# A new order for the opening of a fused attention and gated MLP kernel

## The chip, the cores and the metric

The kernel runs on one core of one Trainium2 chip. The metric is device time in microseconds (us), from a launch's start to its end. The profile is one execution; its engines are PE (TensorE, with PEld for its weight loads), DVE (VectorE), ACT (ScalarE), POOL (GpSimd) and SP (SyncE, which here only issues DMAs).

## The reference

Sliding-window causal attention over 8 batches, 8 heads, 576 positions and head size 64, then an MLP with the gate h·cos(h) on its result:

```python
scores = scale * np.matmul(q, k.transpose(0, 1, 3, 2))
rel = pos[:, None] - pos[None, :]
scores = np.where((rel >= 0) & (rel < 64), scores, -1e9)
attn = softmax(scores)                     # last axis
x = np.matmul(attn, v)                     # to (4608 tokens, 512)
h = x @ w_in                               # 512 -> 2048
return (h * np.cos(h)) @ w_out             # 2048 -> 512, float32
```

## The kernel before, in words

**Tiles.** The 4608 tokens are nine MLP tiles of 512 (`mt`). Tile 0 is positions 0 to 511 of batch 0; tile 1 takes the rest of batch 0 and most of batch 1. From tile 1 on, a loop gives PE its matmuls (L458, L611) and a list of due times (`at`, `pump`) fits in the attention of the next batch. Everything up to there, the opening, is an order written out by hand: the string `FIRST` (L44), which is split at blanks, each word being one step. Each engine executes its own instructions in that order and waits at a step until what it reads has come and what it overwrites is free.

**The steps**, by their letters (the numbers after a letter are a head pair p of 0 to 3 and a half g of tile 0, unless said otherwise; a last letter d, a, p or s is the engine that does it: DVE, ACT, POOL or SP):

- `Lq0.p`, `Lk0.p`: load q, k of batch 0, pair p, cast to bf16 by a DMA issued by POOL (L149). Pair 0 comes by SP in float32 (L155) and is cast by `cq`, `ck`. `Lq1`, `Lk1` load batch 1. `Lv0.c` loads rows of v, 128 positions each (L172); `Lwi`, `Lwo` load quarters of w_in and w_out (L188, L191).
- `io` makes the iota for the masks on POOL (L127), `mk` the masks in five DVE steps (L131 to L135), `mc` casts them to bf16 in three steps on ACT (L139).
- `tq.p`, `tk.p`: 18 small PE transposes of a pair (L200) into PSUM; `pq`, `pk` copy that to SBUF. `Tq`, `Tk`, `Pq`, `Pk` are the same for batch 1.
- `s.p.g.bank`: PE writes the mask into a PSUM bank and adds the scores of four 64-row blocks (L304, L311). `m`: the row max on DVE (L321). `e`: four exps on ACT (L338). `i`: reciprocal on DVE (L348). `n`: the product with it, `w`, on POOL or DVE (L355). `w`: PE transposes it (L371). `c`: copy to SBUF (L121). `Gs`, `Gm`, `Ge` and so on are the same for the groups of batch 1 (there the max and the mask are one DVE operation, L326).
- `zA`, `zB`, `zC`: v is wanted in 128-row windows that begin every 64 rows, so each odd window is put together from halves of the even ones, by a copy between partitions: either an engine's copy (L121) or a DMA from SP (L183). `zA.0`, `zA.1` make the window that half 0 of tile 0 needs, `zB.0`, `zB.1` two that half 1 needs, `zC` one for later.
- `v.a.g`: attention times v for pairs 2a, 2a+1 (L408); `x.a.g` copies that to `xT`, the MLP's input (L121).
- `h.g.f.bank`: the h job f of 0 to 7, eight matmuls (L422). `S` is the sine on ACT (L428), `g` the gate on DVE (L434). `tb` loads ACT's table for it (L453). An h job of half 0 needs x.0.0 and x.1.0; one of half 1 needs x.0.1 and x.1.1.

**Resources that order the steps.** Five single PSUM banks (the last number of `s`, `Gs` and `h`) are taken in turn: a step waits until the bank's last reader is done. Three more PSUM slots (`ps_t`) are shared by tq, tk, Tq, Tk, w and v steps in the order of allocation, so a step waits for the copy that frees the slot three allocations back. A POOL DMA issue waits, on its queue, for the landing of the one eight issues before it.

The copy of v between partitions, with its choice of engine, and the place where FIRST is run:

```python
if engine == "s":
    nc.sync.dma_start(out=to, in_=of)
else:
    copy(engine, to, of)
...
for step in FIRST.split():
    name, *args = step.split(".")
    steps[name](*[int(a) if a.isdigit() else a for a in args])
```

Of the kernel before, what the change touches and what calls it, by code (L numbers as in the profile page):

```python
# [10 lines left out]
def _safe_warn(msg, *a, **kw):  # L11
# [30 lines left out]


FIRST = (  # L44
# [18 lines left out]
)  # L63


# [1 line left out]
def kernel(  # L67
# [10 lines left out]
    B, H, S, D = q.shape  # L78
# [63 lines left out]
    def rows_tile(name):  # L142
        return ld.tile([128, NC * H * D], BF16, tag=name, name=name)

    def load_heads(name, b, p0=0, n=PAIRS):
        if (name, b) not in st:
            st[name, b] = rows_tile(name)[:, 0:PAIRS * RC * D].rearrange("p (a x) -> p a x", a=PAIRS)
        src = {"q": q, "k": k}[name][b, 2 * p0:2 * p0 + 2 * n]
        nc.gpsimd.dma_start(out=st[name, b][:, p0:p0 + n],  # L149
                            in_=src.rearrange("(a h) (p c) d -> (h p) a (c d)", h=2, c=RC))  # L150
# [6 lines left out]
    def cast_plain(name, engine):  # L157
        if (name, 0) not in st:
            st[name, 0] = rows_tile(name)[:, 0:PAIRS * RC * D].rearrange("p (a x) -> p a x", a=PAIRS)
        copy(engine, st[name, 0][:, 0], st.pop(("rows", name)))  # L160

    def load_chunk(name, b, c):
        if (name, b) not in st:
            st[name, b] = rows_tile(name)[0:NP].rearrange("p (c x) -> p c x", c=NC)
        src = {"q": q, "k": k}[name][b, :, c * NP:c * NP + NP]
        nc.gpsimd.dma_start(out=st[name, b][:, c].rearrange("p (h d) -> p h d", h=H),  # L166
                            in_=src.rearrange("h p d -> p h d"))

    def load_v(b, c):
        n = 128 if c < 4 else 64  # L170
        vt = vtiles[b % 2][:n, 2 * c if c < 4 else 2 * c - 1]
        nc.gpsimd.dma_start(out=vt.rearrange("p (h d) -> p h d", h=H),  # L172
                            in_=v[b, :, c * 128:c * 128 + n, :].rearrange("h p d -> p h d"))
# [376 lines left out]
    def spread_first(lo, hi):  # L550
# [2 lines left out]
    steps = {"Lq0": lambda p: load_heads("q", 0, p, 1) if p else load_plain("q"),  # L553
             "Lk0": lambda p: load_heads("k", 0, p, 1) if p else load_plain("k"),
             "cq": lambda engine: cast_plain("q", engine), "ck": lambda engine: cast_plain("k", engine),
             "Lq1": lambda p: load_heads("q", 1, p, 1), "Lk1": lambda p: load_heads("k", 1, p, 1),
             "Lv0": lambda c: load_v(0, c), "Lv1": lambda c: load_v(1, c), "Lq2": lambda c: load_chunk("q", 2, c), "Lk2": lambda c: load_chunk("k", 2, c),
             "Lwi": lambda i: load_w_in(i * d_ff // W_PARTS, (i + 1) * d_ff // W_PARTS),
             "Lwo": lambda i: load_w_out(i * n_ff // W_PARTS, (i + 1) * n_ff // W_PARTS),
# [21 lines left out]
    for mt in range(1, n_mt):  # L581
# [5 lines left out]
        for ff in range(n_ff):  # L587
# [8 lines left out]
            e = ff % 2  # L596
# [54 lines left out]
```

## Time and profile before

| what | value |
|---|---|
| median of three runs | 306.01 us (305.65 to 306.83) |
| the profiled execution | 306.57 us, its span 304.8 us |
| granted TensorE clock in it | 0.999 |
| busy: PE, ACT, DVE, POOL | 293.2, 233.7, 217.4, 195.8 us |
| DMA | 41.44 MB, mean 136 GB/s |

A timeline row gives the start in us from the span's start, the duration, the engine and source line, the operation, what it writes and reads, and in brackets the idle time before it with what ended it; `x6` is six like ones merged, whose duration is then that of the whole run. A row of the chain gives start, duration and the work or wait that the chain went through. A row of a group gives count, total busy time and mean ns. A row of a line's or tile's view gives minimum, median and maximum ns.

### The profile page before, as it was taken

What the parts mean: (1) busy time and instruction counts of PE and PEld (TensorE: products, weight loads), DVE (VectorE), ACT (ScalarE), POOL (GpSimd) and SP (SyncE); (2) the same over time, 40 slices, a digit from 0 to 9 for tenths busy, and PEclk for the clock granted to TensorE, in tenths of its full rate; (3) what the DMA queues carried; (4) which work ended last, traced back from release to release, by engine and by line L of the source; (5) the groups of instructions that cost most, each with busy time, mean ns of one, the idle gap of its engine ahead of it and who ended that gap; (6) DMA issues with size and microseconds to landing.
All of it is one profiled execution on the core that took longest, in us unless ns stands there. A gap on an engine that the chain in (4) does not pass through costs nothing.

```text
span 304.8 us, 8261 instructions
## 1 busy us (share of the span) xinstructions
PE 293.2 (96%) x2840; PEld 154.4 (51%) x2840; DVE 217.4 (71%) x868; ACT 233.7 (77%) x783; POOL 195.8 (64%) x226
## 2 busy tenths in 40 slices
PE   3789999999999999999999999999999999999995
PEld 3667854644455445444544444444544454454443
DVE  3797888898888877787678867886778677236701
ACT  5998699878986799779976998699869986116500
POOL 8899568986999579985998599769804930000000
PEclk9999999999999999999999999999999999999999
DMA  7999999999979995999999999999996852011011
GB/s 144 175 203 184 196 189 142 103 132 169 232 115 115 228 147 80 106 153 233 133 116 150 223 138 109 128 235 148 107 123 147 139 120 98 0 71 69 3 69 69
DMA packets 158186, 41.44 MB, mean 136 GB/s; under 512 B 146944, under 2 KB 153408, under 8 KB 158144
## 3 DMA queue, kind: packets, MB, share of 16 engines
q0 software_dynamic: 100192, 18.06, 80.8%
q1 hardware_dynamic: 57808, 22.66, 40.7%
q8 instruction: 22, 0.36, 0.5%
q14 instruction: 20, 0.16, 0.2%
q10 hardware_dynamic: 144, 0.20, 0.2%
HBM read 36.70 MB, written 9.44 MB: 151 GB/s over the span
## 4 chain that ended last, share of the span: by engine, by line
PE 90%; DVE 3%; DMA 2%; POOL 2%; ACT 1%; issue 1%; POOLq 0%
PE h_ps L458 37%; PE out_ps L611 36%; PE out_ps L441 5%; PE h_ps L422 4%; PE s_ps L289 3%; PE o_ps L390 3%; DMA k<-in_k_dram 2%; PE tq_ps L203 1%; PE out_ps L470 1%; DVE negm L321 1%; POOL q L149 1%; PE s_ps L311 1%; POOL k L149 1%; ACT e L338 0%; DVE wT L121 0%
## 5 line engine op out<-in xcount | busy, mean ns | idle before, releaser
L458 PE MATMUL h_ps<-xT,w_in 128*128 128x512 bf16 x512 | 115.1, 379 | 0.2
L611 PE MATMUL out_ps<-w_out,gT 128*128 128x512 bf16 x496 | 110.0, 379 | 0.0
L600 DVE TENSOR_TENSOR gT<-h_ps,sin 128x512 bf16<-128x512 f32 x128 | 85.1, 688 | 29.3 <-ACT sin L597 28.7
L338 ACT ACTIVATE e<-s,negm 128x128 f32<-128x128 f32 (+1 forms) x256 | 97.2, 382 | 1.7 <-POOL v L121 1.0
L597 ACT ACTIVATE sin<-h_ps 128x512 f32<-128x512 f32 x128 | 73.8, 598 | 31.4 <-PE h_ps L458 30.8
L355 POOL TENSOR_TENSOR w<-e,rden 128x512 bf16<-128x512 f32 (+1 forms) x68 | 69.3, 1033 | 30.8 <-DVE rden L348 25.0
L458 PEld LDWEIGHTS <-w_in 128*128 128x128 bf16 x512 | 48.9, 98 | 54.7
L611 PEld LDWEIGHTS <-gT 128*128 128x128 bf16 x496 | 47.4, 98 | 56.1
L326 DVE CUSTOM_DVE_ANT_0 s<-s_ps,mask 128x128 f32<-128x128 f32 (+1 forms) x256 | 56.1, 277 | 1.7 <-PE s_ps L311 1.4
L338 ACT ACTIVATION_READ_ACCUMULATOR e<-s,negm 128x1 f32 x256 | 48.3, 189 | 0.0
L172 POOL DMA_DIRECT2D v<-in_v_dram x40 | 34.1, 870 | 1.0 <-DMA q<-in_q_dram 1.0
L166 POOL DMA_DIRECT2D q<-in_q_dram x36 | 28.7, 797 | 7.6 <-DMA v<-in_v_dram 2.5
L166 POOL DMA_DIRECT2D k<-in_k_dram x36 | 28.5, 792 | 6.4 <-DMA k<-in_k_dram 4.5
L121 ACT COPY out_sb<-out_ps 128x512 f32<-128x512 f32 (+1 forms) x16 | 9.0, 563 | 23.9 <-PE out_ps L611 18.4
L348 DVE RECIPROCAL rden<-den 128x4 f32<-128x4 f32 (+1 forms) x73 | 12.2, 167 | 19.4 <-ACT e L338 19.0
L121 POOL COPY v<-v 64x1536 bf16<-64x1536 bf16 (+3 forms) x16 | 22.9, 1433 | 0.4
L121 DVE COPY out_sb<-out_ps 128x512 f32<-128x512 f32 x20 | 13.7, 687 | 12.1 <-PE out_ps L611 12.0
L121 DVE CAST xT<-o_ps 128x512 bf16<-128x512 f32 x24 | 15.6, 679 | 8.6 <-PE o_ps L390 8.4
L326 DVE DVE_READ_ACCUMULATOR2_ANT negm<- 128x1 f32 x256 | 21.3, 83 | 0.1
L441 PE MATMUL out_ps<-w_out,gT 128*128 128x512 bf16 x64 | 14.8, 380 | 0.0
L422 PE MATMUL h_ps<-xT,w_in 128*128 128x256 bf16 x128 | 14.6, 273 | 0.0
L422 PEld LDWEIGHTS <-w_in 128*128 128x128 bf16 x128 | 12.3, 98 | 1.4
(67 smaller groups left out, 230.9 us busy)
## 6 DMA issues: line engine op xcount, KB each, us to landing
out_dram<-out_sb SPq DMA_DIRECT2D x16, 512.0 KB, 7.3
v<-in_v_dram POOLq DMA_DIRECT2D x32, 128.0 KB, 6.0
q<-in_q_dram POOLq DMA_DIRECT2D x36, 96.0 KB, 8.7
k<-in_k_dram POOLq DMA_DIRECT2D x36, 96.0 KB, 8.6
w_in<-in_moe_w_in_dram POOLq DMA_DIRECT2D x4, 512.0 KB, 9.2
w_out<-in_moe_w_out_dram POOLq DMA_DIRECT2D x4, 512.0 KB, 11.0
q<-in_q_dram POOLq DMA_DIRECT2D x7, 144.0 KB, 6.5
k<-in_k_dram POOLq DMA_DIRECT2D x7, 144.0 KB, 6.7
```

Source lines behind the costliest of these rows:

```text
L121: {"a": nc.scalar.copy, "p": nc.gpsimd.tensor_copy}.get(engine, nc.vector.tensor_copy)(out, in_)
L166: nc.gpsimd.dma_start(out=st[name, b][:, c].rearrange("p (h d) -> p h d", h=H), in_=src.rearrange("h p d -> p h d"))
L172: nc.gpsimd.dma_start(out=vt.rearrange("p (h d) -> p h d", h=H), in_=v[b, :, c * 128:c * 128 + n, :].rearrange("h p d -> p h d"))
L326: nc.vector.tensor_tensor_reduce(out=s[:, u, c], in0=s_ps[:, u, c], in1=mask[:, 2 - j % 2 if j else 0, c], scale=-scale if b else -1.0, sc ...
L338: nc.scalar.activation(e[:, u, c], s[:, u, c], AF.Exp, bias=negm[:, u:u + 1], scale=1.0 if n < n_first else -1.0, accum_out=den[:, u:u + 1])
L355: (nc.gpsimd if engine == "p" else nc.vector).tensor_tensor(out=w[:, 0:u], in0=e[:, 0:u], op=ALU.mult, in1=rden[:, 0:u].unsqueeze(2).to_br ...
L422: nc.tensor.matmul(out=h_ps[:, half * e:half * e + half], lhsT=w_in_sb[:, ks, ff * 128:ff * 128 + 128], rhs=st["xT", 0][:, ks, half * g:ha ...
L441: nc.tensor.matmul(out=st["out", m], lhsT=st["g", ff // 2][:, ff % 2, m * 128:m * 128 + 128], rhs=w_out_sb[:, ff], start=ff == 0, stop=ff ...
L458: nc.tensor.matmul(out=st["h", ff], lhsT=w_in_sb[:, ks, ff * 128:ff * 128 + 128], rhs=st["xT", mt][:, ks], start=start, stop=stop)
L597: nc.scalar.activation(sin, h_ps, AF.Sin, bias=math.pi / 2.0)
L600: nc.vector.tensor_tensor(out=gt[:, e], in0=h_ps, in1=sin, op=ALU.mult)
L611: nc.tensor.matmul(out=o_ps[e], lhsT=gT[ff // 2][:, ff % 2, ms * 128:ms * 128 + 128], rhs=w_out_sb[:, ff], start=ff == 0, stop=ff == n_ff - 1)
```

## The change

Up to tile 0's sixth h job (`h.0.5`) the order of FIRST is another; what follows is the same. POOL issues five q and k loads before the iota. tq.2 goes ahead of s.0.1, and s.1.1 ahead of s.1.0. Batch 1's pairs 0 and 1 come in one load each for k and q instead of four. The v loads begin with rows 128 to 255. n.0.0 stands among the w_in loads, all four of which now precede n.1.0. s.3.0 and s.2.1 go ahead of batch 1's transposes. zA.0, zA.1 move from DVE to POOL, zB.0 from SP to POOL, zC from SP to DVE; zB.1 stays on SP. n.0.1 moves from POOL to DVE, x.0.0 from ACT to DVE, c.2.1 from DVE to ACT. Gs.9 and Gs.12 change places, and several steps take other banks. The first h job is h.0.1, ahead of w.1.1, w.0.1 and h.0.0.

```diff
 FIRST = (
-    "io Lq0.0 Lk0.0 mk cq.d mc ck.a tq.0 Lq0.1 pq.0.d Lk0.1 tk.0 pk.0.a s.0.0.0 Lq0.2 tq.1 tk.1 m.0.0 pq.1.a s.0.1.1 "
-    "Lk0.2 tq.2 pk.1.d s.1.0.2 Lq0.3 Lk0.3 tk.2 s.1.1.3 e.0.0 tq.3 m.0.1 Lq1.0 Lk1.0 Lq1.1 pq.2.d pk.2.d Lk1.1 tk.3 "
-    "m.1.0 s.2.0.4 Lv0.0 Lv0.1 Tq.0 Lv0.2 pk.3.d m.2.0 e.0.1 pq.3.a i.0.0 e.1.0 Tk.0 s.3.0.0 Tq.1 e.2.0 Lv0.3 Lwi.0 "
-    "Pq.0.d i.1.0 Lwi.1 m.3.0 m.1.1 i.2.0 Pk.0.a e.3.0 Lwi.2 Tk.1 n.1.0.p s.2.1.1 Pq.1.d Gs.10.2 m.2.1 Gs.9.4 "
-    "n.0.0.p Pk.1.a n.2.0.p i.3.0 e.1.1 w.0.0 zA.0.d w.1.0 c.0.0.d Gs.12.0 w.2.0 n.3.0.p i.0.1 c.1.0.d zA.1.d "
-    "c.2.0.d e.2.1 zB.0.s zB.1.s n.0.1.p i.1.1 w.3.0 v.0.0 c.3.0.d x.0.0.a s.3.1.3 Gm.10 v.1.0 m.3.1 i.2.1 Gs.11.2 "
-    "Gm.9 Gm.12 n.1.1.p x.1.0.a e.3.1 w.0.1 w.1.1 c.1.1.a i.3.1 h.0.0.1 h.0.1.4 tb n.2.1.p c.0.1.d Lwi.3 w.2.1 "
-    "h.0.2.0 n.3.1.p v.0.1 S.0.0 Gm.11 w.3.1 S.0.1 h.0.3.3 Lwo.0 S.0.2 c.2.1.d c.3.1.d v.1.1 zC.s g.0.0 S.0.3 "
-    "h.0.4.2 x.0.1.a x.1.1.d h.0.5.1 ...
+    "Lq0.1 Lk0.1 Lq0.0 Lk0.0 Lq0.2 Lk0.3 Lk0.2 io cq.d mk ck.a mc tq.0 pq.0.d tk.0 pk.0.a s.0.0.0 tq.1 tk.1 m.0.0 pq.1.a "
+    "tq.2 s.0.1.1 pk.1.d s.1.1.2 s.1.0.4 tk.2 Lq0.3 m.0.1 Lk1.0.2 Lq1.0.2 e.0.0 pq.2.d i.0.0 m.1.0 pk.2.d tq.3 tk.3 s.2.0.3 "
+    "Lv0.1 Lv0.0 Lv0.2 Lv0.3 e.0.1 pq.3.a pk.3.d m.2.0 s.3.0.0 s.2.1.1 e.1.0 Lwi.0 Tq.0 Tq.1 Tk.0 m.3.0 Lwi.1 n.0.0.p m.1.1 "
+    "i.1.0 Pq.0.d e.2.0 i.2.0 i.0.1 e.3.0 Pk.0.a Pq.1.d m.2.1 Lwi.2 Lwi.3 n.1.0.p Tk.1 i.3.0 n.0.1.d w.0.0 Pk.1.a n.2.0.p "
+    "zA.0.p zA.1.p n.3.0.p e.1.1 Gs.10.4 w.1.0 w.2.0 c.0.0.d c.1.0.d Gs.12.3 v.0.0 w.3.0 e.2.1 Gm.10 i.1.1 c.2.0.d c.3.0.d "
+    "zB.1.s x.0.0.d s.3.1.0 v.1.0 Gs.9.2 m.3.1 Gs.11.1 i.2.1 Gm.11 n.1.1.p zB.0.p zC.d n.2.1.p x.1.0.a e.3.1 h.0.1.4 w.1.1 "
+    "w.0.1 h.0.0.1 w.2.1 i.3.1 Gm.12 c.0.1.d h.0.2.0 c.1.1.a tb n.3.1.p c.2.1.a S.0.0 w.3.1 h.0.3.3 v.0.1 c.3.1.d Gm.9 "
+    "v.1.1 g.0.0 x.1.1.d Lwo.0 S.0.2 S.0.1 x.0.1.a S.0.3 h.0.4.2 h.0.5.1 ...
...
-             "Lq1": lambda p: load_heads("q", 1, p, 1), "Lk1": lambda p: load_heads("k", 1, p, 1),
+             "Lq1": lambda p, n=1: load_heads("q", 1, p, n), "Lk1": lambda p, n=1: load_heads("k", 1, p, n),
```

20 rows, old and new, of the table FIRST are left out of this document.

## The prediction

> **What bounds the kernel now.** I read the page first: the engines' shares and the chain of work that ended last.
>
> ```profile
> PE 293.2 (96%) x2840; PEld 154.4 (51%) x2840; DVE 217.4 (71%) x868; ACT 233.7 (77%) x783; POOL 195.8 (64%) x226
> PE 90%; DVE 3%; DMA 2%; POOL 2%; ACT 1%; issue 1%; POOLq 0%
> ```
>
> TensorE (PE) carries nine tenths of the chain, so the rest is fixed by the amount of matmul work and only the stretch before PE is dense can move. Where that stretch ends is seen in the chain in order of time and in PE's timeline.
>
> ```profile
> 13.00 1.45 issue
> 15.19 1.29 DVE negm L321 x2
> 21.90 1.50 ACT e L338 x8
> 23.90 1.28 ACT L453
> 27.64 10.59 PE h_ps L422 x96
> ```
>
> ```profile
> 21.57 0.62 PE L371 MATMUL tw_ps<-ident,w 128*128 128x128 bf16 x8
> 22.03 1.91 PE L422 MATMUL h_ps<-xT,w_in 128*128 128x256 bf16 x16
> 24.00 1.04 PE L422 MATMUL h_ps<-xT,w_in 128*128 128x256 bf16 x8
> 25.63 0.44 PE L408 MATMUL o_ps<-wT,v 128*64 128x64 bf16 x16 [0.59 <-ACT small L453]
> 27.58 0.83 PE L422 MATMUL h_ps<-xT,w_in 128*128 128x256 bf16 x6
> ```
>
> From 27.58 (h.0.4) PE runs 96 matmuls without a hole. Back from there, to 21.57 (w.0.1 and w.1.1), it does four h jobs, four transposes and two value products with one hole of 0.59 ahead of v.0.1 at 25.63. So the time of this kernel moves with the moment at which this block of PE work begins, plus the holes in it. All my sums are for the start of h.0.4.2, 27.58 now.
>
> The hole is put down to ACT's small operation, but ACT's table load has nothing that v.0.1 reads. Look at the queue that copies v between partitions:
>
> ```profile
> 18.17 2.18 SPq L183 DMA_DIRECT2D v<-v  x3
> DMA to landing us min/median/max: 5.7/6.2/6.6
> ```
>
> Three copies are issued from 18.17 on, some 0.75 apart. The second (zB.1) goes at about 18.9 and lands at most 6.6 later, at 25.5: v.0.1, which needs it, starts at 25.63. So the hole is the landing of a v copy, and it is the one wait that the change surely touches.
>
> **The change part by part.** The start first: masks behind loads.
>
> ```profile
> 1.27 0.53 POOL L127 IOTA mask<- 64x128 f32 x2
> 1.75 0.75 POOL L149 DMA_DIRECT2D q<-in_q_dram  x1
> 4.82 0.55 POOL L149 DMA_DIRECT2D k<-in_k_dram  x1
> 1.83 0.29 DVE L131 TENSOR_TENSOR mask<-mask 128x128 f32<-128x128 f32 x1 [0.96 <-POOL mask L127]
> 3.17 1.02 ACT L139 CAST mask<-mask 128x384 bf16<-128x384 f32 x3 [0.94 <-DVE mask L135]
> 5.86 0.64 ACT L121 COPY kT<-tk_ps 128x576 bf16<-128x576 bf16 x1 [0.78 <-PE tk_ps L200]
> 6.55 0.58 PE L311 MATMUL s_ps<-kT,qT 64*64 64x64 bf16 x8 [0.31 <-ACT kT L121]
> 6.88 0.74 PE L200 MATMUL tq_ps<-ident,q 64*64 64x64 bf16 x18
> 7.47 0.69 PE L200 MATMUL tk_ps<-ident,k 64*64 64x64 bf16 x18
> 11.22 0.45 PE L200 MATMUL tk_ps<-ident,k 64*64 64x64 bf16 x18
> 9.06 0.69 DVE L321 TENSOR_REDUCE negm<-s_ps 128x4 f32<-128x512 f32 x1
> ```
>
> Five load issues now stand before the iota. Five of them run from 1.75 to 4.82, 3.07, so the iota ends at 1.80 + 3.07 = 4.87. DVE's five mask steps and ACT's three casts follow as they do now (iota's end 1.80 to casts' end 4.19, 2.39): 7.26 instead of 4.19. pk.0 stands behind the casts on ACT and ends at 7.26 + 0.58 = 7.84 (0.64 less the overlap with its predecessor), where it ends at 6.50 now. The first scores therefore start at 7.88 instead of 6.55: +1.33. Of the 3.07 delay, 1.74 is hidden in the wait for the first rows and their transposes. What the loads gain by going first: they start 0.48 earlier, but the DMA engines are the same, and no PE step in this stretch waits for them once it is 1.33 late.
>
> Second, tq.2 now goes ahead of s.0.1 on PE: one pair's transposes, 7.47 - 6.88 = 0.59. m.0.1 on DVE, at 9.06 now, comes at 9.06 + 1.33 + 0.59 = 10.98.
>
> From there DVE's queue is full. How closely its steps follow one another:
>
> ```profile
> 11.38 0.68 DVE L321 TENSOR_REDUCE negm<-s_ps 128x4 f32<-128x512 f32 x1
> 11.97 0.75 DVE L121 COPY kT<-tk_ps 128x576 bf16<-128x576 bf16 x1
> 12.64 0.68 DVE L321 TENSOR_REDUCE negm<-s_ps 128x4 f32<-128x512 f32 x1
> 13.23 0.17 DVE L348 RECIPROCAL rden<-den 128x4 f32<-128x4 f32 x1
> 13.32 0.73 DVE L121 COPY qT<-tq_ps 128x576 bf16<-128x576 bf16 x1
> ```
>
> A max takes 0.59 to the next start, a copy 0.67, a reciprocal 0.09. In the new order m.0.1, pq.2, i.0.0, m.1.0, pk.2, pk.3, m.2.0, m.3.0, m.1.1 come before i.1.0: five max, three copies, one reciprocal, 2.95 + 2.01 + 0.09 = 5.05, so i.1.0 starts at 16.03 and ends at about 16.2 (13.96 to 14.13 now by the same queue). ACT starts e.0.1 when m.0.1 ends, 11.67; e.0.1, pq.3 and e.1.0 (1.50 for an exp's four tiles by the chain's row at 21.90, 0.58 for the copy) end at 15.25, so DVE sets it. PE's stall of 1.45 at 13.00 (nothing in the profile ends it; it falls in the middle of a run of transposes) holds s.3.0, m.3.0 and m.1.1 up now. In the new order s.3.0 and s.2.1 stand in front of it, and if it comes after the same number of PE instructions it falls inside Tq.0, near 15.5, where Pq.0 isn't due on DVE until 16.1. So the old stall costs nothing any more; that is why the late masks don't cost their full 1.9.
>
> Third, GpSimd (POOL):
>
> ```profile
> 14.55 0.74 POOL L188 DMA_DIRECT2D w_in<-in_moe_w_in_dram  x1 [0.55 <-DMA q<-in_q_dram]
> 15.37 6.13 POOL L355 TENSOR_TENSOR w<-e,rden 128x512 bf16<-128x512 f32 x6
> L121 POOL COPY v<-v 64x512 bf16<-64x512 bf16 x2 | 2.0, 1012 | 0.1
> L121 POOL COPY v<-v 64x1024 bf16<-64x1024 bf16 x4 | 4.1, 1036 | 0.1
> L121 POOL COPY v<-v 64x1536 bf16<-64x1536 bf16 x5 | 7.3, 1458 | 0.0
> ```
>
> Now n.1.0, n.0.0, n.2.0 and n.3.0 run from 15.37 at 1.02 each (6.13 for six), so n.3.0 ends at 19.45. In the new order n.0.0 is done early, between two w_in loads, Lwi.2 and Lwi.3 stand before n.1.0 (two issues of 0.74, done by about 15.3 with the wait for a q load's landing that the row shows), n.1.0 starts when i.1.0 allows, 16.25, and between n.2.0 and n.3.0 stand the two copies zA. Three norms are 3.06. A copy of 64x512 has no clean row: the two there are took 1.01, but both ran beside a DVE operation in SBUF; the longer shapes lose 0.42 for each 512 elements, which puts it at 0.61. I take 0.8 each, between those: n.3.0 ends at 16.25 + 3.06 + 1.6 = 20.9, with ends of 20.5 and 21.3; +1.45.
>
> DVE's norm (n.0.1) is what these copies would meet:
>
> ```profile
> L355 DVE TENSOR_TENSOR w<-e,rden x5: 681/694/1460, 52.6 to 84.5; 128x512 bf16<-128x512 f32 x4, 128x384 bf16<-128x384 f32 x1
> 84.50 1.46 DVE L355 TENSOR_TENSOR w<-e,rden 128x512 bf16<-128x512 f32 x1
> 83.28 4.22 POOL L121 COPY v<-v 64x1024 bf16<-64x1024 bf16 x4
> ```
>
> It takes 0.69 alone and 1.46 beside POOL's copies. [...] In the sum I let half of it hit POOL (that is the 0.8); the whole is a rival below.
>
> Fourth, from n.3.0's end to the first h job.
>
> ```profile
> 20.58 1.31 ACT L121 CAST xT<-o_ps 128x512 bf16<-128x512 f32 x2
> 20.82 0.44 PE L408 MATMUL o_ps<-wT,v 128*64 128x64 bf16 x16
> ```
>
> Now it is 22.03 - 19.45 = 2.58, of which two x copies stand one after the other on ACT (1.31). x.0.0 goes to DVE, where it costs its 0.6 to m.3.1 and not to this path. w.3.0 0.4, c.3.0 0.4, v.1.0 0.44, x.1.0 0.65 and some 0.2 between them: 2.1. The first h job starts at 20.9 + 2.1 = 23.0.
>
> Fifth, the block. w.0.1 and w.1.1 are behind the first h job instead of ahead of it, so the block begins at 23.0 and not at 21.57: +1.43. The hole of 0.59 goes: zB.1 is now alone on SP and needs only the first three v loads, so it is issued no later than the first copy is now, 18.17, and lands, at 5.7 to 6.6, by 24.8; v.0.1 isn't due before 27. Net +0.84. The block without its hole is 27.58 - 21.57 - 0.59 = 5.42 long, so h.0.4 would start at 28.42. Within it the next late step would be c.2.1, which moves to ACT behind the table load of 1.28: e.3.1 follows x.1.0 and ends near 23.0 + 1.5 = 24.5; c.1.1 (as long as an x copy, 0.65), the load with its small operation (1.5) and c.2.1 (0.65) bring 27.3, and v.1.1, the last 0.44 of the block, is due at 27.98: hidden, by 0.7. I count the last max jobs (Gm.12, Gm.9) as done 0.3 to 1 before their banks are taken; zB.0 on POOL and zC on DVE are off the path. The merged loads for batch 1 save two issues of 0.55 each on POOL, which waits for landings in that stretch anyway: nothing. Lwi.3 goes 8 earlier, which nothing waits for.
>
> Sum: +0.8 to +0.9 on a span of 304.8 and a profiled time of 306.57; that run was 0.56 over the median of the three, 306.01, so I forecast 306.01 + 0.9 = 306.9. About 0.5% of the time, 1.53, is what a measurement of this kernel can tell from no change.
>
> **The rivals.** *Slower: POOL and DVE hold each other up.* Both copies take the 1.01 of the rows and n.0.1 its 1.46, all ahead of c.3.0: n.3.0 ends 0.4 later than in my sum, n.0.1 pushes DVE's c.0.0 to c.3.0 by 0.77, of which the wait for n.3.0 hides 0.4, and x.0.0 and m.3.1 behind them bring e.3.1 past 25.4, where c.1.1, the table load and c.2.1 then reach v.1.1 with no cover: +0.3. Together +0.9 + 0.4 + 0.4 + 0.3 = 2.0: 308.0. For it: every 64x512 copy on POOL in this trace took over 0.95. Against it: both of those met a DVE operation at their start. It decides once n.3.0 ends after 21.5. Chance 0.32.
>
> *Faster: the late start is absorbed.* DVE now idles before 15.19 and PE stalls for 1.45; if PE reaches its faster rate as early as now (a pair's transposes take 0.69 at 7.47 and 0.45 at 11.22) and s.0.1 ends 0.5 sooner, and the copies take 0.5, n.1.0 starts at 15.4, right behind Lwi.3, n.3.0 ends at 19.5, the first h job starts at 21.6, and with the hole gone h.0.4.2 is at 27.0: -0.6, 305.4. To come beyond -1.5 the first h job would have to start at 20.7, which is only possible if the masks don't delay the scores at all. Chance 0.22, of which 0.1 for beyond 0.5%.
>
> *The order changes nothing.* Another wait ends last in both (a weight landing for h.0.2 at 24.00, say): 306.0, chance 0.06. Against it: no PE row in the block names a DMA.
>
> **How the numbers follow.** My case has 0.40: 306.9, from 306.4 to 307.6 by the ends of the copy's price; a sixth of that lies over 307.54. Slower: 0.32 + 0.05, less the part of the rival that stays under (0.02), 0.35. Faster 0.1. The rest, 0.55, is within 0.5%. The range reaches from the faster rival less 0.6 to the slower one plus 0.7: 304.8 to 308.7.
>
> **What would show it.** Right: ACT's mask casts ending near 7.3; the first scores near 7.9; n.1.0 near 16.3 behind DVE's reciprocal; n.3.0 ending near 20.9; the first h job near 23.0 with PE dense from there, and no hole ahead of v.0.1; h.0.4 near 28.4. Wrong: a first h job before 22.5 or after 23.6; a hole in the block that names ACT's c.2.1 or a weight load; or the PE stall of 1.45 on a step that DVE waits for.

## The result: 0.4% longer

The changed kernel takes 307.64 us (median of 22 runs, 306.75 to 309.41), the kernel before 306.19 beside it (22 runs, 305.59 to 307.54). The ratio is 1.0042, 95% interval 1.0030 to 1.0055: 1.3 us longer (1.45 between the medians), clear of the noise but under the 0.5% that the prediction set as the least change to tell. Executions over 1.5% above the fastest of the same kernel stay out of the ratios; only the run "An earlier w_out" has such. The profiled execution took 307.97 us, its span is 306.2 (before: 306.57 and 304.8).

The page of the changed kernel, its engines' shares and the shares of its chain:

```profile
PE 291.2 (95%) x2807; PEld 154.9 (51%) x2840; DVE 217.4 (71%) x868; ACT 233.2 (76%) x783; POOL 196.3 (64%) x226
PE 86%; POOL 3%; ACT 3%; DVE 3%; DMA 2%; issue 2%; POOLq 0%; ACTq 0%
```

No engine's work has changed (33 matmul records are missing, but all 2840 weight loads are there). PE carries less of the chain (86% after 90%), and POOL and ACT more (3% each, after 2% and 1%): the masks on ACT and the copies of v on POOL are now in it. The chain in order of time shows both (start, duration, what):

```profile
6.22 1.02 ACT mask L138 x3
7.24 0.55 ACT kT L120
7.78 0.04 issue
7.83 0.58 PE s_ps L310 x8
...
16.21 0.10 DVE rden L347
16.30 0.07 issue
16.38 0.70 POOL w L354
...
18.41 1.05 POOL v L120
19.46 0.05 issue
19.51 0.62 POOL v L120
20.13 0.07 issue
20.20 1.05 POOL w L354
21.25 0.04 issue
21.30 0.40 PE tw_ps L370 x4
```

The timeline of PE from there:

```profile
23.07 1.05 PE L421 MATMUL h_ps<-xT,w_in 128*128 128x256 bf16 x8
...
27.56 0.69 PE L407 MATMUL o_ps<-wT,v 128*64 128x64 bf16 x32
28.19 1.05 PE L421 MATMUL h_ps<-xT,w_in 128*128 128x256 bf16 x8
```

The first h job starts at 23.07, both value products of half 1 (27.56) follow without a hole, and h.0.4.2 starts at 28.19, where it was at 27.58: +0.61. Set side by side by PE's weight loads, the two traces keep that distance of 0.61 up to 182 us. There, in tile 5's value products (tiles are counted from 0, as above), the changed kernel needs 2.15 instead of 1.20 and so loses another 0.95 (PE's timeline, changed kernel first):

```profile
182.56 0.41 PE L389 MATMUL o_ps<-wT,v 128*64 128x64 bf16 x14
183.27 0.19 PE L389 MATMUL o_ps<-wT,v 128*64 128x64 bf16 x1 [0.30 <-DMA wT<-w]
183.76 0.95 PE L389 MATMUL o_ps<-wT,v 128*64 128x64 bf16 x49 [0.30 <-DMA wT<-w]
```

```profile
181.95 1.20 PE L390 MATMUL o_ps<-wT,v 128*64 128x64 bf16 x64
```

PE waits twice for SP's DMA transposes of the softmax weights (`wT`), which land at 183.2 and 183.7. The traces' landings show what stands around them. The last of the four is issued 0.61 later than in the kernel before, in step with PE, but takes 6.9 to land instead of 5.0 (176.8 to 183.7; before, 176.2 to 181.2). POOL's q and k loads for a later batch are still under way: the last of them lands at 183.5 in the changed kernel and at 180.0 before.

### The profile page after: what moved, and what is told of

The parts are those of the page before. It is cut to its first block, busy times and chain, and to the rows that moved or that the text cites. A ratio compares the mean times of both kernels' runs of the same rounds, so it can differ in the third digit from the quotient of the medians.

```text
span 306.2 us, 8222 instructions
## 1 busy us (share of the span) xinstructions
PE 291.2 (95%) x2807; PEld 154.9 (51%) x2840; DVE 217.4 (71%) x868; ACT 233.2 (76%) x783; POOL 196.3 (64%) x226
## 4 chain that ended last, share of the span: by engine, by line
PE 86%; POOL 3%; ACT 3%; DVE 3%; DMA 2%; issue 2%; POOLq 0%; ACTq 0%
PE h_ps L457 36%; PE out_ps L610 30%; PE h_ps L421 5%; PE out_ps L440 4%; PE o_ps L389 3%; DMA wT<-w 2%; PE s_ps L288 2%; ACT e L337 2%; PE tq_ps L202 1%; PE s_ps L310 1%; POOL w L354 1%; PE out_ps L469 1%; DVE negm L320 1%; PE tw_ps L370 1%; POOL v L120 1%
## 5 line engine op out<-in xcount | busy, mean ns | idle before, releaser
L610 PE MATMUL out_ps<-w_out,gT 128*128 128x512 bf16 x482 | 107.3, 379 | 1.9 <-issue 1.7
L354 POOL TENSOR_TENSOR w<-e,rden 128x512 bf16<-128x512 f32 x67 | 68.2, 1029 | 32.0 <-DVE rden L347 27.3
L120 POOL COPY v<-v 64x1024 bf16<-64x1024 bf16 (+3 forms) x19 | 25.6, 1349 | 0.5
L325 DVE DVE_READ_ACCUMULATOR2_ANT negm<- 128x1 f32 x256 | 21.3, 83 | 0.0
L440 PE MATMUL out_ps<-w_out,gT 128*128 128x512 bf16 x60 | 14.3, 380 | 0.3 <-issue 0.2
```

The lines of the kernel that those rows point to most:

```text
L120: {"a": nc.scalar.copy, "p": nc.gpsimd.tensor_copy}.get(engine, nc.vector.tensor_copy)(out, in_)
L325: nc.vector.tensor_tensor_reduce(out=s[:, u, c], in0=s_ps[:, u, c], in1=mask[:, 2 - j % 2 if j else 0, c], scale=-scale if b else -1.0, sc ...
L354: (nc.gpsimd if engine == "p" else nc.vector).tensor_tensor(out=w[:, 0:u], in0=e[:, 0:u], op=ALU.mult, in1=rden[:, 0:u].unsqueeze(2).to_br ...
L440: nc.tensor.matmul(out=st["out", m], lhsT=st["g", ff // 2][:, ff % 2, m * 128:m * 128 + 128], rhs=w_out_sb[:, ff], start=ff == 0, stop=ff ...
L610: nc.tensor.matmul(out=o_ps[e], lhsT=gT[ff // 2][:, ff % 2, ms * 128:ms * 128 + 128], rhs=w_out_sb[:, ff], start=ff == 0, stop=ff == n_ff - 1)
```

## The experiments

Each was timed in five rounds beside the kernel before. "Full clock" means the executions with a mean granted clock of 0.997 or more; times "at full clock" are means of these.

**The two kernels again.**

> The kernel before once more, for a second profile and as a measure of noise: ratio 1.000 with an interval of some 0.002 to either side. If the 22 runs' difference of 1.45 us is more than the 0.61 by which PE's dense stretch begins later in the two first profiles, then either this profile begins its dense stretch earlier than 27.58 (by up to 0.8), or it has no hole later and the changed kernel has one as a rule.

> The changed kernel once more, for a second profile of it. Theory A (the 0.95 that PE lost at 183 us in the first profile is a chance delay of DMA transposes, in some executions only): PE's start of h.0.4 again near 28.2, with no hole in the value products at 183, or one at another place, and a span near 305.3 without it. Theory B (the new order fills the DMA queues so that the transposes of the fifth batch are always late): the hole at 183 again, 0.5 to 1.5 us.

Before again: 306.52, ratio 0.9994 (0.9959 to 1.0028); changed again: 307.62, ratio 1.0049 (1.0026 to 1.0072). The loss repeats, and so does the hole in tile 5's value products (183.32, 0.70 of it on `wT`), which speaks for theory B; the changed kernel reaches h.0.4.2 at 27.84 this time. But the second profile of the kernel before looks otherwise than the first. Its rows of PE in the block, and its wait at w_out:

```profile
23.27 1.04 PE L422 MATMUL h_ps<-xT,w_in 128*128 128x256 bf16 x8
24.24 0.44 PE L408 MATMUL o_ps<-wT,v 128*64 128x64 bf16 x16
24.85 1.04 PE L422 MATMUL h_ps<-xT,w_in 128*128 128x256 bf16 x8
25.81 0.44 PE L408 MATMUL o_ps<-wT,v 128*64 128x64 bf16 x16
26.19 3.01 PE L422 MATMUL h_ps<-xT,w_in 128*128 128x256 bf16 x26
```

```profile
PE out_ps L441 <- DMA w_out<-in_moe_w_out_dram: 1.2, 1, 1.2
```

The same kernel reaches h.0.4.2 at 26.19, not 27.58, with no hole ahead of v.0.1, and then waits 1.2 at 44 us for w_out's last quarter, landing at 44.75. So here an early opening is taken back. The hole of 0.59 was the landing of zB.1, as the prediction read it (issued at 18.93, landed at 25.54, v.0.1 at 25.63), but it belonged to one execution: in the second profile zB.1 lands at 23.99 and v.0.1 starts at 24.24. The stall at 13.00 isn't fixed either: PE halts at the same instruction, for 0.69 instead of 1.45.

**zB.1 first, in the old order.**

```diff
-zB.0.s zB.1.s n.0.1.p
+zB.1.s zB.0.s n.0.1.p
```

> The kernel before with one edit: on SP the copy zB.1 is issued ahead of zB.0. Theory that the hole of 0.59 ahead of v.0.1 is the landing of a v copy: v.0.1 needs both zB copies, so swapping alone moves little; what binds is the second of the two, whichever it is; the hole stays near 0.5 and the time within 0.2 us. Rival (the hole is ACT's table load, as the profile names it): the same hole, unchanged to 0.05 whatever the order of the copies. If instead only zB.1's own landing mattered, the hole would go and the time fall by 0.4 to 0.6.

306.41, ratio 0.9996 (0.9975 to 1.0017), h.0.4.2 at 26.59 and no hole, where a hole near 0.5 was expected. That is no gain: the repeated kernel before has no hole either, so there was nothing to take.

**The masks ahead of the loads again, in the new order.**

```diff
-Lq0.1 Lk0.1 Lq0.0 Lk0.0 Lq0.2 Lk0.3 Lk0.2 io cq.d
+io Lq0.1 Lk0.1 Lq0.0 Lk0.0 Lq0.2 Lk0.3 Lk0.2 cq.d
```

> The changed kernel with one step moved back: the iota goes ahead of all loads again, as before the change; everything else as changed. Queue theory (late masks pass through DVE's full queue and POOL to the first h job): first scores near 6.6 instead of 7.83, m.0.1 near 9.6 instead of 10.74, i.1.0 near 15.0 instead of 16.12, n.1.0 right behind the w_in issues near 15.0 instead of 16.38, n.3.0 ending near 19.9 instead of 21.25, first h job near 21.9 instead of 23.07: 1.2 us faster than the changed kernel, about 0.1 to 0.6 faster than the kernel before. Rival (the masks' delay is hidden, POOL and ACT set the start of the h jobs anyway): within 0.3 us of the changed kernel, first h job still near 23.

307.51, ratio 1.0048 (1.0020 to 1.0077). n.1.0 starts at 15.22, 1.16 earlier, about as expected; but h.0.4.2 only at 27.62, and the hole at 182 is there. PE's windows (window, its length, PE's busy time and matmuls, granted clock, DMA share, GB/s) show where the rest went:

```profile
17.00:18.00 1.00, 0.64 (x12) 0.93 1.31 225
18.00:19.00 1.00, 1.00 (x10) 0.50 1.15 189
19.00:20.00 1.00, 1.00 (x24) 0.50 1.27 209
20.00:21.00 1.00, 1.00 (x10) 0.50 1.18 244
21.00:22.00 1.00, 1.00 (x28) 0.86 1.24 215
```

For 3.4 us the granted clock is 0.50, and PE's steps in that stretch take longer (sixteen matmuls of a value product 0.64 at 19.34 in it, 0.44 at 21.61 behind it). This execution has a mean clock of 0.994. Of the changed kernel's 34 executions 17 are at 0.993 or 0.994 (their mean time is 308.3, that of the other 17 is 307.3); of the kernel before, beside the experiments, 11 of 110 are under 0.997, and the other 99 have a mean of 306.5. So 0.8 of the loss stands at full clock too. The low clock doesn't explain this run: its seven executions at full clock have a mean of 307.6, no less than the changed kernel's.

**PE kept busy ahead of that stretch.**

```diff
-for c in range(RC):
+for c in [c for _ in range(3 if (name, b, p) == ("k", 1, 0) else 1) for c in range(RC)]:
```

> The changed order with 36 more PE transposes (pair 0 of batch 1's k is transposed three times into the same PSUM slot, ahead of a copy that is later anyway), so that PE works on from 15.9 to 17.3 where it has nothing to do until 16.99. They add work and take none away. Theory (the clock): half of the changed order's executions are granted a mean clock of 0.993 to 0.994 and last 1.0 longer than the others; the granted clock fell to 0.5 from 17.9 to 21.2 in one profile of this kind, behind a stretch of little PE work between 15 and 18. With that stretch filled none or few of the executions show 0.994, and the median comes 0.3 to 0.5 under that of the changed order, 307.2. Rival one: the low clock comes from another stretch (18 to 21.5) or has no tie to PE's work: half of the executions still show 0.994 and the median is 307.6 or more. Rival two: the extra transposes delay Tk.1 and what follows it by their 0.9: 308.3.

307.85, ratio 1.0053 (1.0026 to 1.0080), and 4 of 12 executions at a low clock, against 17 of 34. That settles the theory neither way: PE's busy time from 16 to 17 rose from 0.37 to 0.80, but from 17 to 18 it stayed at 0.63, and the edit opened a new hole in v.0.0 from 20 to 21:

```profile
19.67 0.25 PE L407 MATMUL o_ps<-wT,v 128*64 128x64 bf16 x4
21.02 0.38 PE L407 MATMUL o_ps<-wT,v 128*64 128x64 bf16 x12 [1.10 <-POOL w L354]
```

The wait is put down to a norm that v.0.0 doesn't read. It stands at about PE's 706th instruction (weight loads and matmuls); the stall of 1.45 in the kernel before stands at about its 450th, and both end 1.2 to 1.3 after a packet of 16 KiB lands on q8, a queue that the page lists as `instruction` (13.23 to 14.45, 19.73 to 21.02). In none of the fourteen profiles does the 450th start less than 1.2 after the first such packet has landed, or the 706th less than 1.2 after the second. The 72 instructions that the edit adds bring PE to its 706th sooner; in the changed kernel it starts at 22.27, 2.2 after the second packet's landing at 20.10. That PE waits for these packets is my estimate from these times; no run shows what they hold.

**DMA counts put back.** First batch 1's loads, then the copies, for a theory that the number of DMAs issued in the opening makes the hole.

```diff
-Lk1.0.2 Lq1.0.2
+Lk1.0 Lk1.1 Lq1.0 Lq1.1
```

> The changed order with batch 1's first pairs loaded one by one again, as in the kernel before (four loads of q and k on POOL's queue instead of two). [...] Rival one (the hole comes from when the opening ends, a shift of 0.6 of PE against a DMA schedule): the hole stays, 307.6. [...] The opening itself should not move by more than 0.2 either way, since POOL waits for landings in that stretch.

```diff
-zB.1.s x.0.0.d ... zB.0.p zC.d n.2.1.p
+zB.1.s zB.0.s x.0.0.d ... zC.s n.2.1.p
```

> The changed order with the window copies zB.0 and zC issued by SP again (merged loads kept), so that the number of SP's DMAs is that of the kernel before. Theory (POOL's count matters): the hole near 183 us stays, 307.5. Rival two (SP's count matters): the hole goes and the time is near 306.9. In the opening zB.0 goes out right behind zB.1 on SP, 0.75 later; at 5.7 to 6.6 to landing it is there by 24, before the first half-1 value product needs it near 27, so h.0.4.2 stays within 0.2 of 28.2.

```diff
-Lq1.0 Lk1.0 Lq1.1 pq.2.d pk.2.d Lk1.1
+Lq1.0.2 Lk1.0.2 pq.2.d pk.2.d
```

> The kernel before with only batch 1's first pairs in one load each for q and k. Theory (count of POOL's DMAs): the opening stays within 0.3 of the kernel before, and the hole near 183 us appears, 0.9 to 1.1: 307.0 to 307.4. Rival one (the hole belongs to the late opening): no hole, 306.4. Rival two (SP's count): no hole, 306.4.

With the loads apart the hole is gone from the profile, but the time is 307.56 (1.0047; 1.0030 to 1.0065), at full clock 307.30, where the changed kernel has 307.3. With the copies by SP: 308.09 (1.0058; 1.0038 to 1.0077), no hole at 183 but one in tile 4's value products, and h.0.4.2 at 27.86. The rows of tile 5 in the first, of tile 4 in the second:

```profile
182.48 1.20 PE L389 MATMUL o_ps<-wT,v 128*64 128x64 bf16 x64
```

```profile
152.15 0.98 PE L389 MATMUL o_ps<-wT,v 128*64 128x64 bf16 x51 [0.68 <-DMA wT<-w]
```

The loads merged alone in the old order: 306.36 (0.9996; 0.9973 to 1.0019), no hole, h.0.4.2 at 26.71. So my theory that the count of DMAs makes the hole falls: merged loads don't bring it, and where it goes the median doesn't fall. What fits better is the moment of the opening's end: of the eight profiles that reach h.0.4.2 after 27.6, seven have a wait for `wT`: some 0.6 to 0.8 in five (the changed kernel twice, the masks first and zA on DVE in tile 5, copies by SP in tile 4), 0.2 in two (tiles 1 and 2). Of the six that reach it by 27.6 five have none, and the sixth (an earlier w_out, below) has a cause of its own. The line at 27.6 was drawn after the fact, between 27.58 and 27.62, and seven of the eight have the new order, so order and moment aren't told apart. Nearer to the cause are the loads: in the four profiles with the hole in tile 5 the last q or k load ahead of it lands 0.8 to 1.0 after that tile's value products begin, in the other ten it lands 0.5 or more before. What makes these loads late wasn't found.

**Late masks alone, in the old order.**

```diff
-io Lq0.0 Lk0.0 mk cq.d mc ck.a tq.0 Lq0.1 pq.0.d Lk0.1
+Lq0.0 Lk0.0 Lq0.1 Lk0.1 Lq0.2 Lk0.2 Lq0.3 io mk cq.d mc ck.a tq.0 pq.0.d
```

> The kernel before with only the masks' iota put behind five of the q and k loads, as in the change. My prediction's first step: casts end near 7.3, the first scores near 7.9 (+1.3). Theory: DVE's queue takes that delay on up to the reciprocals (i.1.0 at 15.3 instead of 14.0), and the old hole ahead of v.0.1 stays, since the three copies by SP go as before: h.0.4 comes 0.6 to 1.3 later, 307.0 to 307.8, without the hole near 183 if that hangs on the count of DMAs, and with it (about 308) if it hangs on the moment at which the opening ends. Rival: PE's stall of 1.45 at 13.00 swallows the delay (its end is set by something that does not move with the masks): h.0.4 moves by under 0.3, 306.3 to 306.7.

308.35, ratio 1.0066 (1.0043 to 1.0089), more than the whole change. Here k's cast `ck.a` stands behind the mask casts on ACT, which the change puts ahead of them, so the scores are later still:

```profile
6.14 1.02 ACT L139 CAST mask<-mask 128x384 bf16<-128x384 f32 x3 [3.90 <-DVE mask L135]
7.06 0.67 ACT L121 CAST k<-rows 128x576 bf16<-128x576 f32 x1
```

```profile
9.21 0.58 PE L311 MATMUL s_ps<-kT,qT 64*64 64x64 bf16 x8 [0.31 <-ACT kT L121]
28.59 1.59 PE L422 MATMUL h_ps<-xT,w_in 128*128 128x256 bf16 x13
```

The scores come 2.66 later than before (6.55), h.0.4.2 1.01 later than in the first profile of the kernel before and 2.4 later than in the second. Late masks cost time by themselves in this order, in which they delay the scores twice as much as in the changed one.

**zA on DVE.**

```diff
-zA.0.p zA.1.p n.3.0.p
+zA.0.d zA.1.d n.3.0.p
```

> The changed order with zA.0 and zA.1 on DVE, as in the kernel before, instead of on POOL between n.2.0 and n.3.0. It measures the largest term of my sum, 1.6 for these copies (1.76 in the changed kernel's trace). Theory: n.3.0 ends at 19.4 instead of 21.25, and DVE takes the copies at 19.0, at 0.3 to 0.74 each (their rows before), so DVE's c.3.0 now sets the path: it ends at 21.3 to 21.8 instead of 22.15, the first h job is at 22.2 to 22.7, h.0.4.2 at 27.3 to 27.9, and the time falls by 0.3 to 0.8, to 306.9 to 307.3. Rival one: POOL's norm beside DVE's copies takes as much longer as the copies save, and the first h job stays at 23.0. Rival two: all of the 1.76 comes off, first h job at 21.4, 306.0.

308.12, ratio 1.0062 (1.0038 to 1.0086). POOL's norms, DVE's copies, and the first h job:

```profile
16.38 3.50 POOL L354 TENSOR_TENSOR w<-e,rden 128x512 bf16<-128x512 f32 x3 [1.50 <-DVE rden L347]
18.90 1.45 DVE L120 COPY v<-v 64x512 bf16<-64x512 bf16 x2
```

```profile
24.96 1.76 PE L421 MATMUL h_ps<-xT,w_in 128*128 128x256 bf16 x8
```

n.3.0 ends at 19.88 rather than 21.25, but the first of the two copies takes 1.13 beside it (0.74 in the kernel before) where the second, behind it, takes 0.29, and the norm itself takes 1.40 where the others take 1.03. They stand ahead of DVE's c.0.0 to c.3.0, and this profile's clock is at 0.50 from 19.6 to 26.5, so the first h job comes 1.9 later; how much of that is DVE and how much the clock isn't told apart. The interval overlaps that of the changed kernel: DVE isn't shown to be the better place, nor the worse.

**An earlier w_out.**

```diff
-zB.0.s zB.1.s ... Lq1.0 Lk1.0 Lq1.1 ... Lk1.1 ... Lv1.0 Lwo.1 ... Lwo.3 h.1.7.4 Lv1.1
+zB.1.s zB.0.s ... Lq1.0.2 Lk1.0.2 ... Lwo.1 ... Lwo.3 Lv1.0 h.1.7.4 Lv1.1
```

> The kernel before with three edits: zB.1 ahead of zB.0 on SP, batch 1's first pairs in one load each, and the first v load of batch 1 behind the last quarter of w_out instead of ahead of its second. Theory (what takes an early opening back): in the kernel before the moment at which the opening ends moves between executions, 26.2 to 27.6 for h.0.4, but wherever it is early PE waits at 43 to 45 us for the last quarter of w_out, which lands at 44.2 to 44.8 behind the loads of batch 1 ahead of it (0.4 and 1.2 us of such a wait in the two profiles with the earliest opening). With one v load less ahead of it that quarter lands 0.8 earlier, h.0.4 is at 26.5 to 26.8 and nothing takes it back: span 303.9 to 304.2, median 305.6 to 305.9, ratio 0.997 to 0.998. Rival: w_out's landing does not move, or the batch 1 loads behind it come late in its place: 306.3 to 306.6, ratio 1.000.

Slower than the theory and its rival: five executions lasted 306.96 to 311.52, ratio 1.0081 (1.0033 to 1.0128), the other seven 312.08 to 315.34. The profile is of one of the seven. w_out's last quarter does land earlier, 43.48 (44.75 above), and PE doesn't wait for it. But the last v load and the q loads behind it now wait on POOL for the landings of w_out's quarters, tile 1's norms come later, and SP's six transposes start at 45.43 instead of 43.54 (in the kernel with zB.1 first), the last at 53.5. There they meet batch 2's loads, issued from 52.9 on, and it lands at 59.38:

```profile
59.42 0.66 PE L390 MATMUL o_ps<-wT,v 128*64 128x64 bf16 x30 [3.83 <-DMA wT<-w]
```

**Both early costs undone.**

```diff
-Lq0.1 Lk0.1 Lq0.0 Lk0.0 Lq0.2 Lk0.3 Lk0.2 io cq.d ... tq.2 s.0.1.1 pk.1.d
+io Lq0.1 Lk0.1 Lq0.0 Lk0.0 Lq0.2 Lk0.3 Lk0.2 cq.d ... s.0.1.1 tq.2 pk.1.d
```

> The changed order with two of its edits undone: the masks' iota ahead of the loads, and s.0.1 ahead of tq.2. These are the 1.33 and the 0.59 of my sum that stand at its start. Theory (DVE's queue carries that delay on to the end of the opening): m.0.1 at about 9.1 instead of 10.74, n.1.0 at 14.6 to 15.2 instead of 16.38, n.3.0 ends at 19.5 to 20.1 instead of 21.25, and with a full clock the first h job is at 21.4 to 21.9 and h.0.4.2 at 26.5 to 27.1, as early as in the kernel before; the time is 306.2 to 306.8 in the executions at full clock. [...] Rival two (the start doesn't matter, POOL's copies and norms do): n.3.0 ends after 20.6, 307.3 or more.

306.91 against 307.07 for the kernel before in that comparison: ratio 1.0005 (0.9987 to 1.0024). At full clock 306.93 against 306.99. PE's rows:

```profile
20.08 0.40 PE L370 MATMUL tw_ps<-ident,w 128*128 128x128 bf16 x4 [0.41 <-POOL w L354]
21.86 1.05 PE L421 MATMUL h_ps<-xT,w_in 128*128 128x256 bf16 x8
26.98 1.26 PE L421 MATMUL h_ps<-xT,w_in 128*128 128x256 bf16 x10
```

```profile
181.69 1.38 PE L389 MATMUL o_ps<-wT,v 128*64 128x64 bf16 x64
```

The first h job comes at 21.86 and h.0.4.2 at 26.98, 1.21 and 0.86 earlier than in the changed kernel's two profiles, and tile 5's value products lose only 0.2. So the loss goes with these two edits at the start, and this interval lies below the changed kernel's (1.0030 to 1.0055). It still leaves up to 0.7 us for all the other edits together, and the kernel before took 0.6 to 1.0 more in this comparison than in the others (306.12 to 306.44); the changed kernel wasn't timed in it. In DVE's queue the masks are what counts of the two: i.1.0 starts at 14.91 here and at 14.97 with the masks alone put back (16.12 changed). No version beat the kernel before.

## Why the prediction was right, and where it wasn't

The time lies inside the range (304.8 to 308.7) and within the 0.5% that had the best chance; 306.9 was 0.7 short. (The two ends of the copy's price, 20.5 and 21.3, give 306.5 to 307.3, not the 306.4 to 307.6 named with them.)

*The steps up to h.0.4.2 held.* Casts ended at 7.24 (7.26 in the sum), scores at 7.83 (7.88), m.0.1 at 10.74 (10.98), i.1.0 at 16.12 (16.03), n.1.0 at 16.38 (16.25), n.3.0 ended at 21.25 (20.9), the first h job came at 23.07 (23.0), h.0.4.2 at 28.19 (28.42). DVE's queue, POOL's norms with the two copies, and PE dense from the first h job are what the trace shows:

```profile
16.38 2.03 POOL L354 TENSOR_TENSOR w<-e,rden 128x512 bf16<-128x512 f32 x2 [1.50 <-DVE rden L347]
18.32 0.67 DVE L354 TENSOR_TENSOR w<-e,rden 128x512 bf16<-128x512 f32 x1
18.36 1.76 POOL L120 COPY v<-v 64x512 bf16<-64x512 bf16 x2
21.73 0.42 DVE L120 COPY wT<-tw_ps 128x512 bf16<-128x512 bf16 x1 [0.78 <-PE tw_ps L370]
```

The copies took 1.09 and 0.61, 0.85 each on average, not 0.8: the first runs beside n.0.1, the second doesn't, and 0.61 is the clean price that the prediction worked out from the longer shapes. The slower rival is out: n.0.1 took 0.67, not 1.46, n.3.0 ended before 21.5, and DVE waits 0.78 ahead of c.3.0, so POOL sets the path and DVE has time left. Where the two meet, it is POOL's copy that takes longer beside the norm (1.09 against 0.61, in all seven profiles with this order), not the norm. In the zA run, where POOL's norm starts first, it is the DVE copy (1.13 against 0.29). In both the later starter pays; that this is the rule wasn't tested.

*The term of 0.59 for the hole was mis-sized.* I took it from one profile and called it the one wait that the change surely touches. The same kernel's second profile has no such hole, nor has the one with merged loads and the copies in their old order. Without that credit the sum is +1.43, or 307.4, nearer to the 307.64. The start that the sum counts from is as uncertain: 27.58 is the latest of five profiles of the old opening or near copies of it (26.19, 26.58, 26.59, 26.71), so that the new one's 28.19 and 27.84 are 0.3 to 2.0 later. That the +0.61 between the first two profiles comes near the +0.84 forecast is in part luck.

*tq.2 ahead of s.0.1 was counted whole.* Undoing it moves m.0.1 by 0.35 (9.62 to 9.27), m.1.0 by 0.05 and i.1.0 by 0.06 (14.97 to 14.91), since m.1.0 waits for its own scores. So its share of the delay is hidden, that of the masks isn't.

*"So the rest is fixed by the amount of matmul work" is the step that failed.* In the kernel before, an early opening can be taken back by w_out's landing at 44.2 to 44.8 (waits of 1.2 and 0.4 in two profiles; with zB.1 first PE didn't wait), and a late one met holes at the weights' transposes later (0.95 in the profile). I looked for neither. The faster rival is out for its own reason too: the masks delay the scores by all of 1.28, and n.1.0 starts at 16.38, not 15.4.

*The clock was not in the sum.* Half of the changed kernel's executions have a mean clock that fits one stretch of 3.4 us at half clock, a tenth of the kernel before's. By the means above that is (0.5 - 0.1) x 1.0 = 0.4 of the 1.3; the rest, 0.8, stands between the executions at full clock (307.3 and 306.5). So the low clock adds to the loss and isn't most of it.

What stays open: what makes the half clock more frequent in the new order, what delays the loads at the holes, and why undoing the masks alone (1.0048) is measured so much worse than undoing both (1.0005), when DVE's queue is as early in both. The low clock is not the reason, as the executions at full clock show; the hole in tile 5 may be, and so may noise, since the intervals meet (1.0020 to 1.0077 and 0.9987 to 1.0024).

## What to carry to other kernels

A hole seen in one profile is a term of the sum only if a second profile shows it: here a credit of 0.59 came from one execution alone, and the start of the sum moved by 1.4 between two. Work that every engine needs first (here masks behind five DMA issues) can be dear even when it looks half hidden: a full queue handed the delay on whole (between the masks first and the changed kernel it is 1.12 at the first scores and 1.15 at i.1.0). And a later part that is dense in the profile is so only for the arrival it had, so look up what lands just in time (w_out, the transposes) before you call the rest fixed.

## What the hardware showed

PE stalled at about its 450th instruction in the kernel before (1.45) and at its 706th when 36 transposes, 72 instructions, were added (1.10). Each stall ended 1.2 to 1.3 after a packet of 16 KiB had landed on q8; these packets took 0.97 and 0.96, in stretches in which the profile's DMA share was about 1.2 or more. That the packets are what PE waits for is my estimate, not shown.

The granted clock fell to 0.50 for 3.4 us behind a stretch (14.5 to 17.9, masks first) in which PE's longest hole was 0.84 and PE was busy for 0.55 of the time. With zA on DVE it was 0.50 from 19.6 to 26.5, and PE had been busy for 0.47 of the time from 16 to 19. With an earlier w_out PE had its hole of 3.83 ahead of 59.42, and the mean clock from 60 to 80 was 0.91. So each of these falls had a stretch of little PE work close ahead of it. That such a stretch brings a fall isn't shown: the kernel before was busy for 0.43 of the time from 12 to 15, less than in the first two, and kept a clock of 1.00 up to 28.
